# Softmax weights of a unit moved by three transfers in place of four, with one half of the queries turned by an exchanged identity

## The chip, the cores and the metric

The kernel runs on one core of one Trainium2 chip. The metric is the device time of one execution in microseconds (us), as the median of several runs. An execution that the hardware profiler recorded gives the profile; its span runs from the first to the last instruction of the program.

## The reference

The program is a thresholded attention followed by a feed-forward block. Inputs are q, k, v of shape (8, 8, 576, 64) (batch, heads, tokens, width) in float32, a threshold tau, and the weights w_in (512 x 1024), w_out (1024 x 512) and g_ln (1024) in float64, which the kernel gets as 64-bit words. Cut to what matters:

```python
scores = scale * q @ k.T                     # per batch and head, 576 x 576
thresh = max(scores) - tau
scores = where(scores >= thresh, scores, -1e9)
attn = exp(scores - max(scores)); attn = attn / (sum(attn) + 1e-9)
x = (attn @ v) as (4608, 512)                # heads side by side
h = x @ w_in                                 # 4608 x 1024
solu = h * softmax(h)
ln = (solu - mean) / sqrt(var + 1e-6) * g_ln
out = ln @ w_out                             # 4608 x 512
```

## The kernel before

**Tiling.** Everything is float32. Two heads of a batch make a pair (four pairs a batch). The first 512 tokens of a batch are seen as 128 rows p times 4 tokens t; the last 64 tokens are the "ends". A *slot* is 128 queries of the two heads of a pair against 576 keys: 18 slots a batch (16 from the 512 tokens, in two kinds; two for the ends of all four pairs), 144 in all. Two slots, r = 0 and r = 1, make a *unit*: nine units a batch, 72 in all, of which eight are units of ends (kind 2) and 64 are not.

**TensorE in quarters.** All large products use 64x64 pieces of the array: rows 0 to 63 or 64 to 127 hold the contracted index, columns 0 to 63 or 64 to 127 the output rows. `ROWS` in the code are these two halves.

**One slot, stage by stage.** `scores` (L430) multiplies kT by qT into two PSUM banks, one for each head; output rows 0 to 63 and 64 to 127 (y = 0, 1) are two groups of 64 queries. `maxes` (L462, DVE) takes the row maximum with tau, `ramp` (L486, ACT) and `exps` (L493, ACT) make the thresholded exponentials w, `normalise` (L501, GpSimd) divides by the sum, one round later. `blocks` (L511) then transposes w on DVE in blocks of 32x32 into T: 128 partitions (four groups of 32 queries) by 18 blocks of keys, both slots and both heads.

**From T to wT.** When the second slot of a unit is transposed, four DMAs (L527 to L530), issued from SP, bring T into wT: partition 32a + j of T holds key j of each block for the query group a. A transfer reads 32 partitions of T, 2304 elements each, and writes 64 partitions of wT, 1152 elements each, so that each source row is cut into two. The half of wT (`ROWS[half]`) is the half of 64 queries, g is the group of 32 within it. Each transfer moves 288 KB. `attend_steps` (L534) multiplies v by wT into the bank pv (72 matrix products in a unit, 144 in one of ends): `ROWS[u]` of wT against `ROWS[u]` of v, the two g side by side in the columns. `attended` (L562, ACT) copies pv to xh.

**Turning q and k.** q and k arrive with tokens on partitions and must be turned. `turn` (L312) does that on TensorE: 64 rows of q as the stationary piece, a 64x64 block of the identity `ident` as the moving piece, for both halves r of the 128 rows and both heads. `q_item` (L340) turns q of a pair, scaled on its way out of PSUM: r = 0 by ACT, r = 1 by DVE or ACT. In qT the half r of the token rows becomes the query group y of a slot. k is turned by TensorE for batches 0 and 1 and by DVE transposes and DMAs (`turn_natural`, L186) later. `e_item` turns q of the ends.

**The feed-forward block** follows when 128 tokens are complete: `ff_h` (x times w_in), softmax and normalisation on DVE, ACT and GpSimd, `ff_swap` (L688, four DMAs V<-u), `ff_turn` (a DVE transpose), `ff_o` (times w_out, L715), `ff_out` and `ff_store`.

**What sets the order.** The order on each engine is written out by hand: a loop over rounds (one slot each), in which jobs stand at fixed rounds. A unit's wT is issued in the round after its second slot, its product with v is due three rounds after that slot (`LAG_PV`, L750; four for some). SP's queue issues nearly all DMAs in program order: in the start-up behind a unit's four transfers come the loads of the raw weights (L248, three buffers, converted from 64-bit by DVE, ACT and GpSimd in rounds 0 to 15), then loads of v, q, k, the copies of w2 (L305), V<-u and the stores. The completion semaphores of DMAs are used in turn (eight of them), so that a DMA also waits for the one issued eight earlier. Buffers that the change touches: T has two, wT has two.

**Start.** `constants` (L199) runs on GpSimd, ACT and DVE while the first q and k are loaded: a memset of `lim`, the identity (`make_identity`), memsets of mhalf, mone, zero, then `lim` again when ACT has read it.

Of the kernel before, what the change touches and what calls it, by code (L numbers as in the profile page):

```python
# [8 lines left out]
F32 = mybir.dt.float32  # L9
# [7 lines left out]
P = 128  # L17
# [3 lines left out]
def kernel(  # L21
# [27 lines left out]
    nc = tc.nc  # L49
# [10 lines left out]
    ROWS = (slice(0, 64), slice(64, P))  # L60

    const = ctx.enter_context(tc.tile_pool(name="const", bufs=1))
# [4 lines left out]
    ps_mm = ctx.enter_context(tc.tile_pool(name="ps_mm", bufs=1, space=PSUM))  # L67

    ident = const.tile([P, P], F32, name="ident")
    w1 = const.tile([P, NP, DFF], F32, name="w1")  # L70
    w2 = const.tile([P, 2 * NC, DM], F32, name="w2")
    w1_parts = w1.rearrange("p c (a g x) -> p c g a x", g=2, x=32)
# [126 lines left out]
    def constants():  # L199

        nc.gpsimd.memset(lims[0], 0.0)
        nc.scalar.activation(out=ntau, in_=lims[0], func=AF.Exp)
        make_identity(nc, ident)
        nc.gpsimd.memset(mhalf, -0.5)
        nc.gpsimd.memset(mone, -1.0)
        nc.gpsimd.memset(zero, 0.0)
        for l, e in zip(lims, (916, 896)):
            nc.gpsimd.memset(l, -e * 8388608.0)

        nc.vector.tensor_scalar(
            out=scl, in0=tau_t, scalar1=0.0, scalar2=SCALE, op0=ALU.is_ge, op1=ALU.mult
        )
        nc.vector.tensor_scalar(
            out=tau_t, in0=tau_t, scalar1=0.0, scalar2=104.0, op0=ALU.max, op1=ALU.min
        )
        nc.vector.tensor_scalar(out=ntau, in0=tau_t, scalar1=-1.0, scalar2=None, op0=ALU.mult)
# [90 lines left out]

    SPARE = 7  # L310

    def turn(spare, x, lhsT_of, rows=2):  # L312

        o = spare["base"] + 64 * x
        to = slice(o, o + 64)
        for r in range(rows):
            for y in range(2):
                nc.tensor.matmul(
                    out=spare[r][ROWS[y], to], lhsT=lhsT_of(r, y), rhs=ident[ROWS[r], ROWS[r]],
                    start=True, stop=True,  # L320
                )

    def seen(spare, r, x, n):
        o = spare["base"] + 64 * x
        return spare[r][:, o : o + 64 * n].rearrange("p (t k) -> p t k", t=n)

    def source(i):
        b, hp = divmod(i, NP)
        return halves[b, hp // 2], 2 * (hp % 2)

    def pair(i):
        if i not in pairs:
            pairs[i] = dict(
                qT=heads.tile([P, SM], F32, tag="qT", bufs=6, name="qT"),
                kT=heads.tile([P, S], F32, tag="kT", name="kT"),
                qe=heads.tile([P, ST], F32, tag="qe", name="qe"),
            )
        return pairs[i]

    def q_item(i, ts=slice(0, 4)):  # L340
        src, h0 = source(i)
        qT = pair(i)["qT"].rearrange("p (t r k) -> p r t k", t=4, r=2)
        n = ts.stop - ts.start

        def make(spare, x):
            for t in range(n):
                turn(spare, x + t, lambda r, y: src["q"][ROWS[r], h0 + y, ts.start + t])

        def keep(spare, x, r):
            if r == 0 or spare.get("eased"):  # L350
                nc.scalar.activation(
                    out=qT[:, r, ts], in_=seen(spare, r, x, n), func=AF.Copy, scale=scl
                )
            else:
                nc.vector.tensor_scalar(
                    out=qT[:, 1, ts], in0=seen(spare, 1, x, n), scalar1=scl, scalar2=None,
                    op0=ALU.mult,
                )

        return n, make, keep  # L360
# [5 lines left out]
    def k_item(i, ts=slice(0, 4)):  # L366
        src, h0 = source(i)
        to = k_parts(i)
        n = ts.stop - ts.start

        def make(spare, x):
            for t in range(n):
                turn(spare, x + t, lambda r, y: src["k"][ROWS[r], h0 + y, ts.start + t])

        def keep(spare, x, r):
            (nc.vector.tensor_copy if r and not spare.get("eased") else nc.scalar.copy)(
                out=to[:, 4 * r + ts.start : 4 * r + ts.stop],
                in_=seen(spare, r, x, n).rearrange("p t (k c) -> p t c k", c=2),
            )

        return n, make, keep

    def e_item(i):
        src, h0 = source(i)
        last = k_parts(i)[:, NK - 1] if i < 2 * NP else None

        def make(spare, x):
            turn(
                spare, x, lambda r, y: ends[i // NP][ROWS[r], 2 * (i % NP) + y],
                2 if i < 2 * NP else 1,  # L390
            )

        def keep(spare, x, r):
            if r == 0:
                nc.scalar.activation(
                    out=pair(i)["qe"], in_=seen(spare, 0, x, 1)[:, 0], func=AF.Copy, scale=scl
                )
            elif last is not None:
                (nc.scalar.copy if spare.get("eased") else nc.vector.tensor_copy)(
                    out=last, in_=seen(spare, 1, x, 1)[:, 0].rearrange("p (k c) -> p c k", c=2)  # L400
                )

        return 1, make, keep
# [107 lines left out]
    def blocks(s):  # L511
        b, kind, hp, r = slots[s]
        key = (b, kind, hp)
        if r == 0:
            units[key] = dict(T=work.tile([P, NB, 2, 2, 32], F32, tag="T", name="T"))
        u = units[key]
        T = u["T"]
        for h, w in enumerate(live.pop(s)["w"]):
            nc.vector.transpose(out=T[:, :, r, h, :], in_=w)  # L519
        if r == 0:  # L520
            return


        T = T.rearrange("p (c m) r h x -> p c (m r h x)", c=2)
        u["wT"] = wT = work.tile([P, 2, NK, 2, 2, 32], F32, tag="wT", bufs=2, name="wT")
        to = wT.rearrange("p g m r h x -> p g (m r h x)")
        for g in range(2):  # L527
            for half in range(2):
                of = 64 * half + 32 * g
                nc.sync.dma_start(out=to[ROWS[half], g], in_=T[of : of + 32])  # L530
# [278 lines left out]
    with tc.manual_schedule():  # L809
        nc.scalar.dma_start(out=tau_t, in_=tau.partition_broadcast(P))  # L810
        load_qk(0, 0)
        weight_load(0)
        constants()
        for x in range(1, 3):
            weight_load(x)
# [23 lines left out]
        while True:  # L839
# [115 lines left out]
            if attending is not None:  # L955
# [3 lines left out]
                b, kind, hp = attending  # L959
# [4 lines left out]
            if rnd - 1 in live:  # L964
                blocks(rnd - 1)
# [6 lines left out]
            if rnd in pieces:  # L972
                x = pieces[rnd]
# [44 lines left out]
```

## Time and profile before

| what | value |
|---|---|
| median of 3 runs | 881.4 us (881.29 to 883.73) |
| the profiled execution | 883.54 us |
| its span | 881.8 us, 38016 instructions |
| granted TensorE clock, mean | 0.980 |
| wT<-T | 288 DMAs of 288 KB, issued by SP |
| T<-w (L519, DVE) | 288 transposes, 752 ns each |
| pv<-wT,v (L555, TensorE) | 5760 products, 170.9 us busy |
| s_ps<-ident,q (L318, TensorE) | 896 products, 224 ns each |
| tp<-ident,q (L318, TensorE) | 128 products, 314 ns each |
| memory traffic | HBM read 46.14 MB, written 9.44 MB; DMA 161.60 MB in all |

How to read the profile. PE is the matrix product of TensorE, PEld its load of the stationary piece, DVE VectorE, ACT ScalarE, POOL GpSimd, SP SyncE, whose only work here is to issue DMAs ("SPq"). A line such as `PE pv L555 <- DMA wT<-T: 3.7, 6, 1.3` says that TensorE sat idle before instructions of line 555 writing pv, that a DMA writing wT from T ended this, and gives the sum in us, the number of times and the longest. Matrix products overlap, so busy time is that of the engine, while the mean duration of one counts its whole passage. The DMA share is the mean busy share of 16 DMA engines; it can be a little over 1 where packets overlap. The granted clock is TensorE's, as a share of full speed.

### The profile page before, as it was taken

To read this page: it belongs to the slowest core of one execution; us is meant where nothing else is said; L and a number is where in the kernel's file an instruction comes from. 1 tells how busy PE (TensorE), PEld (TensorE's weight loads), DVE (VectorE), ACT (ScalarE), POOL (GpSimd) and SP (SyncE) were. 2 spreads that over 40 slices of the span, in tenths; PEclk is the share of its full clock that TensorE was granted. 3 is DMA by queue.
4 is the path that set the end of the run, shared out by engine and by line. 5 is a ranking of instruction groups with operands and counts; after the bars stand their busy time and mean duration, and the time that the engine had idled before them with its cause. 6 is when DMAs were issued, how large, how long until landed. Compare 5 with 4: busy or idle time off the path is not lost. (4 is left out here: it accounts for less than half of the span.)

```text
span 881.8 us, 38016 instructions
## 1 busy us (share of the span) xinstructions
PE 835.4 (95%) x16225; PEld 592.1 (67%) x16225; DVE 682.0 (77%) x1248; ACT 586.3 (66%) x1201; POOL 471.0 (53%) x888
## 2 busy tenths in 40 slices
PE   5667999989999999999999999999999999999997
PEld 3445666665676877677777777777677677777655
DVE  5989788878787888888778887888687888777451
ACT  5977777767666766767677677777676777775121
POOL 2878655545555555555554655555555555555120
PEclk9878899999999999999999999999999999999999
DMA  7999978887878796988789787888779777866222
GB/s 230 254 260 256 218 186 196 217 191 175 201 170 212 178 208 157 206 207 189 158 194 214 184 204 166 208 213 185 165 173 219 182 174 155 186 133 143 65 49 49
DMA packets 85033, 161.60 MB, mean 183 GB/s; under 512 B 19832, under 2 KB 49536, under 8 KB 84864
## 3 DMA queue, kind: packets, MB, share of 16 engines
q1 hardware_dynamic: 83728, 157.18, 76.6%
q8 instruction: 127, 2.08, 1.1%
q10 hardware_dynamic: 1136, 2.00, 0.7%
q14 instruction: 42, 0.34, 0.1%
HBM read 46.14 MB, written 9.44 MB: 63 GB/s over the span
## 5 line engine op out<-in xcount | busy, mean ns | idle before, releaser
L473 DVE CUSTOM_DVE_ANT_0 w<-s_ps,tau_t 128x576 f32<-128x576 f32 x280 | 200.7, 754 | 108.0 <-PE s_ps L451 90.7
L715 PE MATMUL o_ps<-w,uT 64*64 64x256 f32 x4608 | 265.2, 376 | 1.1 <-DVE uT L703 1.1
L488 ACT ACTIVATE w<-s_ps,nth 128x576 f32<-128x576 f32 x280 | 199.8, 743 | 97.0 <-DVE nth L473 93.1
L715 PEld LDWEIGHTS o_ps<-w,uT 64*64 64x64 f32 x4608 | 218.9, 133 | 58.3 <-issue 13.8
L507 POOL TENSOR_SCALAR w<-w,sm 128x576 f32<-128x576 f32 x288 | 218.8, 772 | 14.3
L497 ACT ACTIVATE w<-w,ntau 128x576 f32<-128x576 f32 x288 | 220.3, 772 | 0.0
L611 PE MATMUL h_ps<-w,xh 64*64 64x512 f32 x1856 | 220.0, 596 | 0.0
L519 DVE STREAM_TRANSPOSE T<-w 128x576 f32<-128x576 f32 x288 | 206.3, 752 | 7.4 <-POOL w L507 6.0
L555 PEld LDWEIGHTS pv<-wT,v 64*64 64x64 f32 x5760 | 166.5, 136 | 51.1 <-issue 36.3
L451 PE MATMUL s_ps<-kT,qT 64*64 64x64 f32 (+1 forms) x2048 | 168.1, 422 | 16.4 <-ACT w L488 12.5
L555 PE MATMUL pv<-wT,v 64*64 64x128 f32 (+1 forms) x5760 | 170.9, 263 | 7.9 <-DMA wT<-T 3.7
L611 PEld LDWEIGHTS h_ps<-w,xh 64*64 64x64 f32 x1856 | 98.3, 135 | 96.6 <-issue 88.6
L504 POOL TENSOR_SCALAR sm<-sm 128x2 f32<-128x2 f32 x144 | 36.0, 250 | 229.5 <-ACT w L497 226.4
L505 POOL TENSOR_TENSOR sm<-sm,mone 128x2 f32<-128x2 f32 x144 | 104.6, 726 | 12.0
L677 ACT ACTIVATE V<-u,nb,rs 128x1024 f32<-128x1024 f32 x36 | 44.7, 1241 | 52.2 <-POOL nb L667 52.2
L451 PEld LDWEIGHTS s_ps<-kT,qT 64*64 64x64 f32 x2048 | 61.8, 139 | 25.1 <-ACT w L488 17.7
L578 ACT COPY xh<-pv 128x256 f32<-128x256 f32 x64 | 23.7, 370 | 67.3 <-PE pv L555 67.3
L703 DVE STREAM_TRANSPOSE uT<-V 128x1024 f32<-128x1024 f32 x36 | 44.5, 1236 | 23.7 <-DMA V<-u 23.5
L497 ACT ACTIVATION_READ_ACCUMULATOR w<-w,ntau 128x1 f32 x288 | 56.9, 198 | 0.0
L635 ACT ACTIVATE u<-h_ps,hm 128x1024 f32<-128x1024 f32 x36 | 40.2, 1118 | 21.2 <-DVE hm L626 15.3
L626 DVE TENSOR_REDUCE hm<-h_ps 128x1 f32<-128x1024 f32 x36 | 43.1, 1197 | 12.2 <-PE h_ps L611 6.2
L682 DVE TENSOR_SCALAR u<-u,rs,nb 128x1024 f32<-128x1024 f32 x36 | 42.4, 1178 | 12.7 <-ACT V L677 12.4
(82 smaller groups left out, 590.4 us busy)
## 6 DMA issues: line engine op xcount, KB each, us to landing
wT<-T SPq DMA_DIRECT2D x288, 288.0 KB, 5.9
v<-in_v_dram SPq DMA_DIRECT2D x48, 288.0 KB, 4.8
V<-u SPq DMA_DIRECT2D x144, 64.0 KB, 4.1
out_dram<-ob SPq DMA_DIRECT2D x71, 128.0 KB, 3.1
q<-in_q_dram SPq DMA_DIRECT2D x15, 512.0 KB, 5.9
k<-in_k_dram SPq DMA_DIRECT2D x96, 72.0 KB, 4.6
kT<-flip SPq DMA_DIRECT2D x48, 144.0 KB, 2.7
raw<-in_moe_w_out_dram SPq DMA_DIRECT2D x8, 512.0 KB, 8.2
```

The costliest lines, as they stand in the source:

```text
L451: nc.tensor.matmul(out=ps[h][ROWS[y], ks], lhsT=lhsT, rhs=d["kT"][ROWS[h], ks], start=True, stop=True,)
L473: nc.vector.tensor_tensor_reduce(out=w, in0=ps[:, 0:S], in1=(zero if loose else tau_t).to_broadcast([P, S]), scale=1.0, scalar=BIG, op0=AL ...
L488: nc.scalar.activation(out=d["w"][x], in_=d["w"][x] if d["loose"] else d["ps"][x][:, 0:S], func=AF.Prelu, bias=d["nth"][x], scale=-1.0, al ...
L497: nc.scalar.activation(out=w, in_=w, func=AF.Exp, bias=ntau, scale=1.0, accum_out=sm[:, x : x + 1])
L505: nc.gpsimd.tensor_tensor(out=sm, in0=sm, in1=mone, op=ALU.pow)
L507: nc.gpsimd.tensor_scalar(out=w, in0=w, scalar1=sm[:, x : x + 1], scalar2=1.0, op0=ALU.mult, op1=ALU.mult)
L519: nc.vector.transpose(out=T[:, :, r, h, :], in_=w)
L555: nc.tensor.matmul(out=to, lhsT=d["v"][ROWS[u], h0 + h, m ^ 4 * u if m < 8 and b < 2 else m], rhs=rhs, start=m == 0, stop=m == NK - 1,)
L611: mm = nc.tensor.matmul(out=h[ROWS[y], f], lhsT=x[ROWS[r], c, ROWS[y]], rhs=w1_parts[ROWS[r], c, part ^ r], start=part == 0 and c == 0, st ...
L677: nc.scalar.activation(out=V, in_=u, func=AF.Identity, bias=nb, scale=rs)
L703: nc.vector.transpose(out=uT, in_=d["V"].rearrange("p y (m x) -> p m y x", x=32))
L715: nc.tensor.matmul(out=d["o"][ROWS[z], 512 * r : 512 * r + 256], lhsT=d["uT"][ROWS[r], m].rearrange("p y x -> p (y x)"), rhs=w2[ROWS[r], m ...
```

## The change

`blocks` issues three transfers for a unit that is not of the ends. The first reads partitions 32 to 95 of T (64 rows of 2304 elements) and writes all 128 rows of wT for g = 1 (1152 elements each), 576 KB. The other two read partitions 0 to 31 and 96 to 127 and write g = 0 of the two halves, 288 KB each. In the second half this puts T's partitions 64 to 95 into g = 1 and 96 to 127 into g = 0, the other way round than before. So that the columns of the product with v keep their tokens, the two groups of 32 queries in the second half are exchanged when q is turned: `turn` uses, for r = 1 and with `swap` set, `swapped`, a 64-column tile in which the two 32-column blocks of the identity's lower half stand exchanged. `swapped` is made once, by two GpSimd copies of 64 x 32 right behind the identity. `q_item` sets `swap`; `k_item` and `e_item` don't. Units of the ends keep their four transfers.

```diff
     ident = const.tile([P, P], F32, name="ident")
+    swapped = const.tile([P, 64], F32, name="swapped")
...
         make_identity(nc, ident)
+        for g in range(2):
+            of = 64 + 32 * (1 - g)
+            nc.gpsimd.tensor_copy(
+                out=swapped[ROWS[1], 32 * g : 32 * g + 32], in_=ident[ROWS[1], of : of + 32]
+            )
         nc.gpsimd.memset(mhalf, -0.5)
...
-    def turn(spare, x, lhsT_of, rows=2):
+    def turn(spare, x, lhsT_of, rows=2, swap=False):
...
                 nc.tensor.matmul(
-                    out=spare[r][ROWS[y], to], lhsT=lhsT_of(r, y), rhs=ident[ROWS[r], ROWS[r]],
+                    out=spare[r][ROWS[y], to], lhsT=lhsT_of(r, y),
+                    rhs=swapped[ROWS[1]] if swap and r else ident[ROWS[r], ROWS[r]],
                     start=True, stop=True,
                 )
...
             for t in range(n):
-                turn(spare, x + t, lambda r, y: src["q"][ROWS[r], h0 + y, ts.start + t])
+                turn(
+                    spare, x + t, lambda r, y: src["q"][ROWS[r], h0 + y, ts.start + t], swap=True
+                )
...
         to = wT.rearrange("p g m r h x -> p g (m r h x)")
+        if kind < 2:
+            nc.sync.dma_start(out=to[:, 1], in_=T[32:96])
+            for half in range(2):
+                nc.sync.dma_start(out=to[ROWS[half], 0], in_=T[96 * half : 96 * half + 32])
+            return
         for g in range(2):
             for half in range(2):
                 of = 64 * half + 32 * g
```

## The prediction

> **What bounds the kernel now.** I read the busy shares first, then the slices, then one table by stage. The busy shares and the slices, as the page has them:
>
> ```profile
> PE 835.4 (95%) x16225; PEld 592.1 (67%) x16225; DVE 682.0 (77%) x1248; ACT 586.3 (66%) x1201; POOL 471.0 (53%) x888
> ...
> PEclk9878899999999999999999999999999999999999
> DMA  7999978887878796988789787888779777866222
> ```
>
> TensorE is busy for 835.4 of 881.8 us, so all that can be won without taking work from it is 46.4 us. The slices say where those lie: the first five of 40 (0 to 110 us) have the low clock digits and the full DMA engines. The table by stage (length; busy time and count of PE, PEld, DVE, ACT, POOL; granted clock; DMA share; GB/s) makes it exact:
>
> ```profile
> 0.00:20.00 20.00, 10.22 (x190) 6.45 (x194) 9.13 (x24) 10.86 (x26) 4.62 (x17) 1.00 0.80 250
> 20.00:40.00 20.00, 15.11 (x289) 9.95 (x281) 19.54 (x43) 17.86 (x41) 16.86 (x20) 0.83 0.94 238
> 40.00:60.00 20.00, 12.80 (x194) 8.86 (x192) 17.70 (x37) 13.06 (x28) 15.33 (x19) 0.74 1.04 250
> 60.00:100.00 40.00, 30.58 (x494) 20.87 (x498) 36.04 (x72) 32.74 (x71) 31.10 (x42) 0.83 1.04 256
> 100.00:200.00 100.00, 95.53 (x2018) 68.23 (x2014) 78.64 (x153) 70.87 (x151) 54.79 (x105) 0.98 0.84 197
> ...
> 500.00:600.00 100.00, 100.00 (x2037) 71.06 (x2033) 81.51 (x148) 70.03 (x145) 54.52 (x106) 1.00 0.85 199
> ```
>
> From 100 us to about 850 TensorE has no room: 100.00 busy in 100.00. DMA engines at 0.85 beside it cost nothing. In the start-up, 20 to 100 us, TensorE is idle for 80 - (15.11 + 12.80 + 30.58) = 21.5 us. There DVE is busy for 73.3 of 80 us and the DMA engines have a share of about 1: DVE converts the 64-bit weights beside its attention work, and the weights, the batches and the blocks of wT all pass the DMA engines. So the start-up is bound by DVE, with DMA just behind it.
>
> Third, the waits that end on a transfer (sum, times, longest). Those of the whole span:
>
> ```profile
> PE s_ps L451 <- ACT w L488: 12.5, 14, 2.8
> ...
> DVE uT L703 <- DMA V<-u: 23.5, 21, 4.1
> ...
> PE pv L555 <- DMA wT<-T: 3.7, 6, 1.3
> ...
> DVE em L259 <- DMA raw<-in_moe_w_out_dram: 1.6, 1, 1.6
> ```
>
> The changed transfers hold TensorE for 3.7 us in six places: 0.2 us in 40 to 60, 2.1 in 60 to 100, 1.3 in 100 to 300 and 0.2 in 300 to 500. DVE waits for raw weights 1.6 us at 57.85 and 0.5 us at 46.43. The 12.5 us on `ACT w L488` are score banks that come free when DVE and ACT have read them, which is the DVE bound seen from TensorE.
>
> Last, how the four transfers of a unit lie in time, from SP's own timeline in the start-up and the DMA table (KB each, median us from issue to landing):
>
> ```profile
> 44.58 4.60 SPq L530 DMA_DIRECT2D wT<-T  x4
> 49.50 1.93 SPq L248 DMA_DIRECT2D raw<-in_moe_w_out_dram  x2
> 54.75 3.58 SPq L530 DMA_DIRECT2D wT<-T  x4
> 58.42 4.83 SPq L248 DMA_DIRECT2D raw<-in_moe_w_out_dram  x2
> ```
>
> ```profile
> wT<-T SPq DMA_DIRECT2D x288, 288.0 KB, 5.9
> ```
>
> Four issues take 3.58 us, 0.9 us apart, and each lands 5.9 us after its issue: about 2.7 + 5.9 = 8.6 us from the first issue to the last landing. Raw weights are queued right behind.
>
> **What the Trainium skill says.** (1) "SBUF — State Buffer", section "Door 1: The DMA port swizzle": partitions 0 to 63 reach the same eight of sixteen ports that 0 to 31 reach, and 64 to 127 reach the other eight. So each of the four transfers now reads and writes through eight ports alone; the new one reads 32 to 95 and writes 0 to 127, sixteen ports on both sides. (2) "DMA: Bandwidth & Descriptors", section "Rules for kernel authors": two transfers to disjoint partition halves serialize, and one transfer over 128 partitions should replace them. The page by itself does not say that 32 to 95 as source does as well. The trace of before agrees with both as far as it can: 288 KB every 0.9 us would be 328 GB/s, but in the stages from 40 to 100 us, where the DMA engines have no idle time, they move only 250 to 256 GB/s over all. At the page's 27.2 GB/s a port, 288 KB through eight ports take an estimated 1.36 us, four of them 5.4, and one of 576 KB through sixteen again 1.36 us.
>
> **The change part by part.**
>
> *Transfers.* In 64 units (eight batches, two kinds, four pairs) four transfers become three; the eight units of the ends keep four. That is 64 issues fewer. Bytes are the same. One issue is worth 3.58 / 4 = 0.9 us of SP, so what stands behind a unit on SP's queue (raw weights, the copies of w2, V<-u, v, k, q) is issued up to 0.9 us earlier. If the issue of 576 KB takes as long as two, the saving is nothing; the 512 KB loads of `raw` (0.33 to 0.36 us each when nothing is ahead) say that bytes don't set it. I take 0.9.
>
> *DMA engines.* By the estimate above a unit takes 4 x 1.36 = 5.4 us of full DMA time now and 3 x 1.36 = 4.1 after. No row of the trace shows a 64-to-128 transfer of such rows without others around it, so the two ends are: nothing gained (128 written rows, dealt out so that two engines meet on one port, as now), and 1.36 us a unit. In 20 to 100 us there are seven units (issued at 24.5, 34.4, 44.6, 54.8, 66.8, 78.8, 91.2): 0 to 9.5 us of DMA time. I take most of it, so the DMA share of the steady stage falls from about 0.83 to 0.72: 64 x 1.36 us over the some 800 us in which the units lie is 0.11.
>
> *TensorE.* `rhs` of q's second half is a 64x64 block of another tile: the same count (x896 on s_ps, x128 on tp), the same shape, 224 and 314 ns. Cost 0. Scores and pv multiply the same shapes; the exchanged rows only order their columns.
>
> *GpSimd.* Two copies of 64x32 behind `make_identity`. The nearest rows: a MEMSET of 128x128 takes 204 ns, one of 128x1 98 ns, a two-input operation of 128x1 196 ns. So 0.2 to 0.6 us for both. Queued behind them are three MEMSETs (1.27 to 1.43 us now) and those of `lim` (at 4.65 us, released by ACT), and TensorE's first turn waits for k until 6.02 us. These 3 us hide it; were that cover gone, 0.6 us would be on the path.
>
> *What it is worth.* After 100 us TensorE is the bound, so only its own waits count: 1.3 + 0.2 us on wT. With the last block landing 0.9 to 2.3 us earlier and the longest of these waits 1.1, they go: -1.3 (0.2 left for what is next, the pv banks freed by ACT). In the start-up DVE is the bound. Its 2.1 us on raw weights: the raw tile at 57.85 has three units ahead of it, 3 x 1.36 = 4 us of DMA time, more than the 1.6 it waits. What is late next is GpSimd's scaling (15.33 of 20 us busy in that stage; 0.7 us of DVE waits on it) and the score banks, so I count 1.2 of the 2.1. TensorE's 2.3 us on wT in the start-up count only where DVE then waited for scores (1.6 us): 0.5. Sum: 1.3 + 1.2 + 0.5 = 3.0 us. V<-u lands earlier too, but DVE's 23.5 us on it are idle time of an engine that isn't the bound; only 1.1 us of TensorE's (uT, at the end) come from it, and that is behind the last unit.
>
> The profiled execution took 883.54 us, a span of 881.8 and 1.7 around it, and lies 2.1 us above the median of 881.4. The 3.0 us are a difference in that execution; I take them from the median: 881.4 - 3.0 = 878.4.
>
> **The rivals.**
>
> *A, likeliest: ports and issues both relieve the start-up*, 878.4. Its own range: 881.4 - 1.5 - 2.1 - 2.3 = 875.5 if every wait on these transfers is won (and a little below if a stretch of halved clock goes with them), to 880.2 if half of the 3.0 is lost.
>
> *B: hidden.* The large transfer takes as long as the two it replaces, since engines meet on the written side, and only the issue is saved. Speaking for it: TensorE is 100% busy, DVE has 6.7 idle us in the start-up. Then 0.9 us of earlier landing takes away the 0.2 and about half of 1.3 after 100 us: 881.4 - 0.8 = 880.6, between 879.5 and 882.5.
>
> *C: slower.* The 576 KB transfer lands later than the two did, because its 128 written rows are dealt out so that engines collide on ports, and pv waits for all three. The point from which it decides is the room between the last landing and pv. One unit of the steady stage: issues from 405.25 to 408.74, last landing some 5.9 us after 408.1, pv at 415.55: 1.5 us of room there, and none in the start-up, where pv waits already. If blocks land 1 us later than now, each of the seven units of the start-up holds TensorE 1 us longer, and the scores that stand behind pv on TensorE reach DVE, the bound, that much later: 7 us, of which I take 2 as hidden by DVE's weight work. So 881.4 + 5 = 886.4. Against it: bytes and rows are the same, and the eight-port transfers collide already.
>
> **How the numbers follow.** A 0.50, B 0.30, C 0.20. This kernel's measurement tells 0.3%, 2.6 us, from no change: faster is below 878.8, slower above 884.0. A gives 0.42 faster and 0.08 same; B 0.03 faster, 0.24 same, 0.03 slower; C 0.02 same and 0.18 slower. Together 0.45, 0.34, 0.21. Range 875.0 to 886.0: all of A, all of B, and nearly half of C, with 0.1 to 0.15 left out.
>
> **What would show it.** A: wT in 224 issues; a unit's issues in about 2.7 us; the DMA share near 0.72 from 100 to 700 us; no `em <- raw` wait over 0.5 us; waits of pv on wT below 1 us; PE busy unchanged within 3 us. B: the DMA share above 0.8 in those stages. C: pv waits on wT above 5 us, or a median landing of the 576 KB transfer above 8 us. The forecast is wrong if the start-up isn't shorter although the DMA share fell (DVE alone bound it), or if clock windows in it move by more than all this.

## The result, and the profile after

The changed kernel took 880.1 us in the median (876.61 to 884.24, 22 runs), the kernel before, timed beside it, 883.42 us (878.83 to 887.85, 22 runs). The ratio is 0.9951, with a 95% interval of 0.9934 to 0.9968: faster by 0.5%, some 4 us. The profiled execution has a span of 878.3 us against 881.8. One of the profiles taken later (three transfers in the second and third batch alone) is of an execution 1.3% longer than the median of its kernel, so only that kernel's ratio is used below.

Busy shares and slices of the changed kernel:

```profile
PE 831.3 (95%) x16225; PEld 585.2 (67%) x16225; DVE 680.0 (77%) x1248; ACT 586.8 (67%) x1201; POOL 471.0 (54%) x890
...
PEclk9878899999999999999999999999999999999999
DMA  7999877887877777887778786887678776765322
```

TensorE's count is the same and its share too. GpSimd has its two more instructions, and in sum the same 471.0 us of busy time. Only the DMA digits are lower nearly everywhere. The table by stage of the changed kernel (columns as in the prediction):

```profile
20.00:40.00 20.00, 14.29 (x289) 9.10 (x281) 19.54 (x42) 17.82 (x41) 16.90 (x20) 0.79 0.94 250
40.00:60.00 20.00, 14.04 (x196) 10.26 (x196) 18.91 (x40) 14.28 (x30) 16.77 (x20) 0.66 1.04 258
60.00:100.00 40.00, 30.26 (x478) 18.48 (x482) 34.67 (x69) 31.46 (x69) 29.20 (x42) 0.83 0.98 247
100.00:200.00 100.00, 95.81 (x2042) 71.51 (x2038) 79.60 (x156) 72.29 (x154) 56.51 (x107) 1.00 0.81 199
...
500.00:600.00 100.00, 100.00 (x2048) 70.45 (x2044) 82.29 (x149) 70.53 (x145) 54.49 (x106) 1.00 0.80 198
```

From 500 to 600 us nearly the same bytes pass (198 GB/s, 199 before) with a DMA share of 0.80 in place of 0.85. Over 100 to 700 us, the kernel before and then the changed one:

```profile
100.00:700.00 600.00, 591.12 (x12013) 424.49 (x12009) 483.80 (x886) 420.53 (x863) 328.80 (x639) 1.00 0.83 191
```

```profile
100.00:700.00 600.00, 591.69 (x12114) 420.67 (x12110) 484.28 (x889) 423.11 (x868) 330.57 (x643) 1.00 0.78 192
```

In the start-up this pair of profiles shows no gain. DVE, the engine that bounds it, is busy for 19.54 + 18.91 + 34.67 = 73.1 us of 20 to 100 us, 73.3 before: what 40 to 60 us has more, 60 to 100 us has less. The waits of the changed kernel that answer to those shown of before:

```profile
DVE uT L717 <- DMA V<-u: 9.0, 7, 4.1
...
PE pv L569 <- DMA wT<-T: 3.5, 3, 1.6
...
DVE em L265 <- DMA raw<-in_moe_w_out_dram: 1.3, 2, 0.9
...
PE s_ps L460 <- ACT qT L360: 0.9, 1, 0.9
```

The last of them has a counterpart in the kernel before that the prediction does not show:

```profile
PE s_ps L451 <- ACT qT L351: 2.5, 1, 2.5
```

TensorE's wait on wT is hardly less in sum, but all of it now lies before 100 us (1.6 us at 63 us, 1.4 and 0.6 at 76 us). DVE's wait for V<-u fell from 23.5 to 9.0 us. SP's timeline and the DMA table of the changed kernel:

```profile
44.30 0.59 SPq L537 DMA_DIRECT2D wT<-T  x1
44.94 2.90 SPq L539 DMA_DIRECT2D wT<-T  x2
47.94 2.94 SPq L254 DMA_DIRECT2D raw<-in_moe_w_out_dram  x2
54.20 0.58 SPq L537 DMA_DIRECT2D wT<-T  x1
54.83 3.23 SPq L539 DMA_DIRECT2D wT<-T  x2
```

```profile
wT<-T SPq DMA_DIRECT2D x160, 288.0 KB, 6.5
wT<-T SPq DMA_DIRECT2D x64, 576.0 KB, 5.4
```

The large transfer is issued in 0.6 us and lands after 5.4 us in the median, where half of it took 5.9; but the two small ones behind it hold SP for 2.9 and 3.2 us. In the start-up (20 to 100 us) the three issues of a unit take 3.3 to 4.2 us, the four of before 3.5 to 4.6.

### The profile page after: what moved, and what is told of

Same layout as the page of the kernel before. It is cut to its first block, busy times and chain, and to the rows that moved or that the text cites. A ratio compares the mean times of both kernels' runs of the same rounds, so it can differ in the third digit from the quotient of the medians.

```text
span 878.3 us, 37901 instructions
## 1 busy us (share of the span) xinstructions
PE 831.3 (95%) x16225; PEld 585.2 (67%) x16225; DVE 680.0 (77%) x1248; ACT 586.8 (67%) x1201; POOL 471.0 (54%) x890
## 5 line engine op out<-in xcount | busy, mean ns | idle before, releaser
L625 PE MATMUL h_ps<-w,xh 64*64 64x512 f32 x1856 | 217.3, 592 | 0.0
L569 PEld LDWEIGHTS pv<-wT,v 64*64 64x64 f32 x5760 | 164.0, 136 | 50.5 <-issue 39.5
L569 PE MATMUL pv<-wT,v 64*64 64x128 f32 (+1 forms) x5760 | 167.5, 263 | 6.8 <-DMA wT<-T 3.5
L625 PEld LDWEIGHTS h_ps<-w,xh 64*64 64x64 f32 x1856 | 94.3, 134 | 98.4 <-issue 95.5
L655 DVE TENSOR_TENSOR u<-h_ps,u 128x1024 f32<-128x1024 f32 x36 | 42.8, 1190 | 11.3 <-ACT u L649 11.3
```

Of the source, the lines that this page charges most:

```text
L569: nc.tensor.matmul(out=to, lhsT=d["v"][ROWS[u], h0 + h, m ^ 4 * u if m < 8 and b < 2 else m], rhs=rhs, start=m == 0, stop=m == NK - 1,)
L625: mm = nc.tensor.matmul(out=h[ROWS[y], f], lhsT=x[ROWS[r], c, ROWS[y]], rhs=w1_parts[ROWS[r], c, part ^ r], start=part == 0 and c == 0, st ...
```

## The experiments

Each was timed beside the kernel before on the same chip; a ratio below 1 is faster. Theory 1, formed on the two profiles: the gain comes after the start-up, where DVE waits for V<-u that lands late behind wT, and TensorE behind DVE. Theory 2, the prediction's: the start-up is shorter, and some waits on wT are gone. Beside them stands the question whether sixteen ports or fewer transfers do it.

**The kernel before once more** (no edit).

> The kernel before, unchanged, once more: a control for what a comparison of this size can tell, and a second profile. All theories: ratio 1.000 within the noise (a few tenths of a per cent). If the stalls are the program's own and not chance, the profile again has TensorE's wait of about 2.5 us for qT near 180 us (with DVE waiting for V<-u ahead of it) and a wait on wT of about 1.3 us near 235 us. If they are chance, they stand elsewhere or nowhere.

Ratio 1.000 (0.9982 to 1.0018). TensorE waits for qT again near 180 us, 1.7 us this time, and on wT near 235 us, 1.1 us: the program's own waits, of varying size.

**The changed kernel once more** (no edit).

> The changed kernel once more. Ratio to before 0.995 (about -4 us). Theory 1 (tight places after the start-up): DVE's waits for V<-u near 9 us in sum in place of 23.5, no stall over 1.5 us at 180 us, the first 100 us as long as before. Theory 2 (the start-up is shorter, as predicted): TensorE reaches the products of the second batch 1 to 2 us earlier than before by 105 us.

Ratio 0.9959 (0.9940 to 0.9979): the gain stands. DVE's wait for V<-u is 9.1 us, TensorE's for qT 0.9 us in both profiles of this kernel. So what theory 1 asked of the waits came true, and TensorE reaches the end of the start-up only 0.6 us earlier than in the second profile of before (109.3 against 109.9 us, at a mark explained below), less than theory 2 asked.

**Three transfers in the first batch alone.** `few(b)` replaces the condition in `blocks` and sets `swap`:

```diff
+    def few(b):
+        return b == 0
...
-        if kind < 2:
+        if kind < 2 and few(b):
```

> Three transfers and exchanged rows in the first batch alone, four elsewhere. Theory 1: no gain, ratio 0.999 to 1.001, and the waits for V<-u stay near 23 us. Theory 2 (start-up): at least half of the gain, ratio about 0.997.

Ratio 0.9959 (0.9941 to 0.9977). DVE's wait for V<-u stayed at 20.4 us, and the gain was there. This speaks for theory 2 and against theory 1.

**Three transfers in the second and third batch alone** (`return 0 < b < 3`).

> Three transfers and exchanged rows in the second and third batch alone (about 105 to 330 us), four elsewhere. Theory 1: most of the gain, ratio about 0.996, -3 us in TensorE's time between 130 and 290 us. Theory 2: 1.3 us from waits on wT, ratio about 0.9985.

Ratio 0.9970 (0.9947 to 0.9994): a gain too, between what the two theories had; the interval holds both. Together the two parts give more than the whole change, which the intervals allow; so they don't share the gain out.

**Four of the eight batches, before and changed.** The edit is the same in both:

```diff
     B, H, S, D = q.shape
+    B = 4
```

> The kernel before, cut to the first four of eight batches (the other half of the output isn't computed). It ends at about 460 us. All theories: only its difference to the changed kernel cut alike counts; the next run says how much.

> The changed kernel, cut to the first four of eight batches. Theory 1 and theory 2 (the gain lies in the start-up and the first tight places, before 330 us): the whole gain, 3 to 4 us less than the run before this. Rival (every unit gains a little, all along): half of it, about 2 us.

484.38 us (480.95 to 486.08, 4 runs) and 479.78 us (478.71 to 482.77, 4 runs): 4.6 us less in half of the work. That favours a gain in the first half over one in every unit, and no more: with four runs each, the two ranges overlap, and 2 us is not excluded.

**No V<-u, before and changed.**

```diff
-                middle.setdefault(rnd + 3, []).append(lambda t=cur: (ff_norm2(t), ff_swap(t)))
+                middle.setdefault(rnd + 3, []).append(lambda t=cur: ff_norm2(t))
```

> The kernel before without the 144 transfers V<-u (the feed-forward block then works on rows that weren't exchanged), so nothing waits for them and they take no DMA time. Theory 1 (V<-u, which lands late behind wT, holds DVE, and through it TensorE): faster by 3 us or more, ratio 0.9965 or less. Theory 2 (DVE's waits for V<-u are idle time that costs nothing): within 1 us, ratio 0.999 to 1.001.

> The changed kernel without the transfers V<-u. Theory 1: close to the run before this, within 1.5 us, since what the three transfers gave is given already. Theory 2: still 3 to 4 us faster than the run before this.

0.9965 (0.9947 to 0.9982, median 883.38 us) and 0.9926 (0.9895 to 0.9957, 878.38 us). The first number alone would fit theory 1. The second speaks against it: with nothing left to wait for at V<-u, the change still gives 5.0 us between the medians, where theory 1 had at most 1.5. With 7 runs of the second kernel the two intervals just overlap, so the size is rough. V<-u costs the kernel some 3 us by itself, which theory 2 had at nothing, and that is another matter.

**Exchanged rows with four transfers.** The large transfer is cut by partitions:

```diff
-            nc.sync.dma_start(out=to[:, 1], in_=T[32:96])
+            for half in range(2):
+                of = 32 + 32 * half
+                nc.sync.dma_start(out=to[ROWS[half], 1], in_=T[of : of + 32])
```

> Exchanged rows and the two GpSimd copies as in the change, but four transfers of 32 partitions each, in the changed arrangement. All theories: the exchange itself costs and gives nothing, ratio 0.998 to 1.002, and transfers as before: a DMA share near 0.81 in 100 to 700 us.

Ratio 0.9997 (0.9978 to 1.0015), DMA share 0.83 in 100 to 700 us, as before (0.83). The exchange and GpSimd's copies cost nothing that can be told.

**Three transfers, the large one through half of the ports on its read side.**

```diff
-            nc.sync.dma_start(out=to[:, 1], in_=T[32:96])
+            nc.sync.dma_start(out=to[:, 1], in_=T[0:64])
             for half in range(2):
-                nc.sync.dma_start(out=to[ROWS[half], 0], in_=T[96 * half : 96 * half + 32])
+                of = 64 + 32 * half
+                nc.sync.dma_start(out=to[ROWS[half], 0], in_=T[of : of + 32])
```

> Three transfers as in the change, but the large one reads partitions 0 to 63 (the small ones 64 to 95 and 96 to 127), so that it reads through half of the ports; the rows of the blocks land in the wrong places, the amount of work is the same. If the ports make the gain: ratio 0.998 or above, DMA share near 0.81, landing as before. If the number of transfers makes it: ratio 0.995 to 0.997, as the change.

Ratio 1.0080 (1.0052 to 1.0108): slower by 7 us. Its waits (sum, times, longest):

```profile
PE pv L570 <- DMA wT<-T: 6.0, 8, 1.8
...
DVE em L265 <- DMA raw<-in_moe_w_out_dram: 4.0, 1, 4.0
...
PE s_ps L460 <- ACT qT L360: 3.1, 1, 3.1
...
DVE em L265 <- DMA raw<-in_moe_w_in_dram: 2.0, 1, 2.0
```

In 100 to 700 us:

```profile
100.00:700.00 600.00, 589.36 (x11968) 431.45 (x11964) 481.23 (x882) 420.57 (x864) 328.42 (x633) 1.00 0.83 191
```

What the change eased is not eased here: the DMA share is that of before, there are eight waits on wT in place of six, and DVE waits 6.0 us for raw weights in place of 2.1 (3.8 in the second profile of before). The number of transfers is that of the change. Fewer transfers don't make the gain; which partitions they read matters. One thing is left untested: the two small transfers of this kernel both read partitions of the upper half, in the change one reads the lower and one the upper, and that may be a part of the loss.

**Four transfers, two of them through all ports.**

```diff
-            nc.sync.dma_start(out=to[:, 1], in_=T[32:96])
+            for z in range(2):
+                cols = slice(576 * z, 576 * z + 576)
+                nc.sync.dma_start(out=to[:, 1, cols], in_=T[32:96, :, cols])
```

> Four transfers: the large one of the change cut into two by columns, both from partitions 32 to 95 to all 128 rows (rows of 2304 in place of 4608 bytes), then the two small ones. If the ports make the gain: ratio 0.995 to 0.997, DMA share 0.77 or a little above. If the number of transfers makes it: ratio 0.999 to 1.001.

Ratio 0.9972 (0.9949 to 0.9995), DMA share 0.76 in 100 to 700 us (0.78 with the change). With as many transfers as before, but this half through all ports, a gain is there, though its interval comes close to 1. SP issues each of the four in 0.6 us in the median, less time for a unit than in the change, and the kernel is no faster for it.

**Three transfers in the last five batches alone** (`return b > 2`).

> Three transfers and exchanged rows in the fourth to eighth batch alone, four transfers in the first three. If the gain lies before 330 us, where TensorE waits for blocks and for qT: ratio 0.999 to 1.001. If every unit gives a little: 5/8 of the gain, ratio 0.997 to 0.998.

Ratio 0.9988 (0.9964 to 1.0013), although five of eight batches have the change, the DMA share is 0.80 and DVE's wait for V<-u 11.3 us. No gain can be told, and TensorE waits for next to nothing of it there (0.2 us on wT after 300 us in the profile of before). The interval still holds the 0.997 to 0.998 of a small gain in every unit.

**Where in the span.** Two instructions mark the stages in each profile: the first product of `o_ps` (the end of the start-up) and the first with `xe` (about 270 us). The lines give count, durations in ns (least, median, most), first and last start in us. The kernel before:

```profile
L715 PE MATMUL o_ps<-w,uT x4608: 376/376/427, 108.3 to 876.3; 64*64 64x256 f32 x192
```

```profile
L611 PE MATMUL h_ps<-w,xe x192: 586/589/640, 270.8 to 684.2; 64*64 64x512 f32 x192
```

The changed kernel:

```profile
L729 PE MATMUL o_ps<-w,uT x4608: 375/376/427, 108.6 to 873.2; 64*64 64x256 f32 x192
```

```profile
L625 PE MATMUL h_ps<-w,xe x192: 588/589/590, 268.8 to 680.9; 64*64 64x512 f32 x192
```

One pair of profiles would mislead: here the start-up is 0.3 us longer. Over all profiles:

| profile | first o_ps | first xe | last o_ps |
|---|---|---|---|
| before | 108.3 | 270.8 | 876.3 |
| before, again | 109.9 | 270.1 | 875.9 |
| before, four batches | 108.9 | 271.2 | 474.1 |
| before, no V<-u | 111.4 | 272.2 | 876.8 |
| exchanged rows, four transfers | 110.9 | 271.0 | 877.0 |
| three transfers in the last five batches | 112.3 | 273.8 | 878.8 |
| changed | 108.6 | 268.8 | 873.2 |
| changed, again | 109.3 | 267.5 | 872.0 |
| changed, four batches | 108.5 | 267.3 | 473.5 |
| changed, no V<-u | 110.0 | 268.4 | 874.5 |
| three transfers in the first batch | 109.2 | 267.9 | 875.7 |
| four transfers, two through all ports | 109.6 | 267.8 | 879.3 |
| three transfers, half of the ports | 114.5 | 276.4 | 886.4 |

The six without wide transfers up to 270 us have means of 110.3 and 271.5. The six with them in the first batch have 109.2 at the first mark, and the five of those that have them in the next two batches as well 268.0 at the second. So of 3.5 us some 1.1 come from the start-up and 2.4 from 109 to 270 us. Estimated from the spread of these twelve profiles, the first has a standard error of 0.7 us and is not clear of chance; the second, with 0.5, is. Behind that, the two profiles of before need 605.5 and 605.8 us to the last product, those of the changed kernel 604.4 and 604.5; but the other whole kernels of the table lie between 604.6 and 611.5 there, and in the four-batch pair 3.3 of the 3.9 us won by 270 us are lost again by the end. So nothing is read from that stretch.

Between the two marks, the same products keep TensorE busy for 155.7 us in the mean of the first six profiles and for 154.7 in the mean of the other six; it is idle for 5.5 and 4.0 us. Of the 1.5 us of idle time, 0.7 are waits on wT (0.2 to 1.3 in the first six, none in the others), 0.4 waits for qT (1.4 and 1.0 in the mean) and 0.4 waits of q's turn for DVE (1.4 and 1.0). About half of the 1.0 us of busy time comes from two profiles (before; before, four batches), in which the granted clock is 0.66 and 0.69 from 180 to 185 us, right behind the wait for qT.

## Why the prediction was right, point by point

**The bound.** Right in the main. TensorE is still busy 95% of the span, 500 to 600 us still 100.00 of 100.00 us, and a lower DMA share behind 330 us alone gave nothing that can be told (the last five batches). But "from 100 us on no room" was a misreading: in the row 100 to 200 of the prediction's own table TensorE is busy for 95.53 of 100 us, and most of the gain lies between 109 and 270 us.

**The sum.** 3.0 us were forecast; the two medians differ by 3.3 us, the spans by 3.5, and the ratio says 0.5% (0.3 to 0.7). The parts did worse than the total. The start-up was put at 1.7 us and measures about 1.1, with a spread of 4 us between single profiles of kernels that have four transfers in the first batch. In the mean of the six profiles on each side, DVE's wait for raw weights in it fell from 4.0 to 2.1 us, more than the 1.2 counted, and DVE's waits for GpSimd rose from 0.9 to 1.7, as the prediction had expected of what is late next; but TensorE's wait on wT didn't fall (2.7 and 3.0 us), so the 0.5 us counted for it didn't come. The 1.3 us for waits on wT after 100 us was the value of one profile: between 104 and 290 us it is 1.3, 1.1 and 0.8 us in three profiles of the kernel before (whole, again, four batches), but 0.2 to 0.3 in three other kernels with four transfers there. That these waits go was right: none is left there in any profile of the changed kernel. That the total came so close is in part luck, as the terms that came out too large are made up by one that is missing.

**What was missing in the sum.** The rest of the 2.4 us between 109 and 270 us. TensorE waits for qT near 180 us 2.5, 1.7 and 1.3 us in the same three profiles of before, 0.9 us in all of the changed kernel. In the first of them DVE has waited 1.5 us for V<-u at 176.5 us, and only behind the work that follows does ACT come to qT; in the changed kernel that wait is gone. The prediction called DVE's waits for V<-u idle time without cost; at this place, in this profile, it isn't. But in the mean over the six profiles on each side this gives no more than some 0.4 us, TensorE's wait for qT was also as low as 0.9 in the kernel with exchanged rows and four transfers, and the two kernels without V<-u speak against the gain hanging on it. In the first profile of before this wait was followed by the stretch of lower granted clock (32 products of h_ps in 5.38 us in place of 3.65), which made it look like the main cause.

**The signs.** Of those listed for A, the 224 issues came true and the others didn't: a unit's issues take 3.3 to 4.2 us in the start-up and not 2.7, the DMA share is 0.78 and not 0.72, the longest waits on raw weights and on wT are 0.9 and 1.6 us, and TensorE's busy time fell by 4.1 us. By the prediction's last sign, a start-up that isn't shorter although the DMA share fell, the first pair of profiles would even have spoken against it (108.6 us against 108.3, with a share of 0.99 against 1.02 in 20 to 100 us). What speaks for the start-up is the kernel with the change in the first batch alone (0.9959), though in its one profile, too, more is won behind the first mark than before it.

**Issues.** The step "one issue is worth 0.9 us of SP" failed. The issue of the large transfer takes 0.6 us, but those behind it 1.4 us in the median, where one of before takes 0.6 in the median and 0.9 in the mean. What SP waits for there isn't shown by the trace; that SP's time for a unit stayed nearly the same is. The 512 KB loads that I took as proof that bytes don't count were not issued with nothing ahead, as the prediction has it: the one at 40.72 us took 0.33 us while three transfers of wT were still to land. So neither bytes nor transfers in flight set that one issue.

**Ports.** The direction was right, the size not. By the port map of the Trainium skill's "SBUF — State Buffer" ("Door 1: The DMA port swizzle"), partitions 32 to 95 reach all sixteen ports, and the runs agree in kind: all ports 0.9951 and 0.9972, half of them 1.0080, with equal bytes. That the partitions read decide is what the runs show; that it is by their ports is the page's account. But the share of the steady stage fell by 0.05 (0.83 to 0.78 in 100 to 700 us), not by the 0.11 estimated from the page's 27.2 GB/s a port. So a unit wins about half of the 1.36 us (an estimate: 0.05 of 600 us, over the 48 units of that stretch, is 0.6 us). "DMA: Bandwidth & Descriptors" ("Rules for kernel authors") advises one transfer in place of two on disjoint halves; the kernel with half of the ports shows that one transfer in place of two is not enough, since it was slower than two.

**Rival B (hidden)** fell with the ratio's interval. **Rival C (slower)** didn't come true for the change, but a merged transfer can lose: with half of the ports on the read side TensorE and DVE wait longer for wT and the raw weights, the start-up is 4.2 us longer (114.5 us in its one profile, against a mean of 110.3), and the ratio of 1.0080 is 7 us. That this is near the 5 of C is no proof of C's mechanism, which was a late landing by the written side: the written side is that of the change, and the large transfer lands after 5.6 us in the median, against 5.4.

**GpSimd and TensorE** cost nothing that can be told, as the exchanged rows alone show.

**What stays open.** The kernel with the change in the first batch alone also stands at 267.9 us at the second mark, with four transfers in each unit after it, and has no wait on wT between the marks; whether the start-up leaves the queues in a better order, or chance does, wasn't settled. Nor why the gain by ports is only half, nor what makes three transfers with half of the ports slower than four: its profile loses some 4 us behind 276 us as well (610.0 us to the last product, 605.5 and 605.8 before).

## What to carry to other kernels

When SBUF-to-SBUF transfers come from a few partitions, look at which ports each side reaches, and try one transfer that straddles partition 64; an exchange of rows that an earlier matrix product does for nothing can make that possible. Price such a gain only at the places where the bound engine waits for these transfers or for what is queued behind them, and look for these places in every row of the table by stage; here they were the start-up and the 160 us behind it. And before a single pair of profiles is read as the cause, take a second pair: the largest wait of the first was partly chance.

## What the runs showed that was not expected

A merged transfer doesn't save its issue here: three issues took 3.3 to 4.2 us in the start-up where four took 3.5 to 4.6. And merging can lose: three transfers with the large one read from partitions 0 to 63 were 0.8% slower than four of 32 partitions. V<-u, only 9.4 of 161.6 MB, costs about 3 us (0.9965, 0.9947 to 0.9982, without it).
